# Cross-attention with a feed-forward block on one core: identity built by VectorE, output blocks in place, spread weight differences, and another order for x's loads and transposes

## Chip, cores and metric

The kernel runs on one core of one Trainium2 chip. The metric is the device time of one execution in microseconds (us), as a median of several executions. Beside it stands the span of the profiled execution, from its first to its last instruction; it is some 1.8 us shorter than the time of the same execution. PE is TensorE, PEld its weight load, DVE VectorE, ACT ScalarE, POOL GpSimd, SP SyncE. A run is called slow when its time is over 1.5% above the fastest of the same kernel; comparisons use the others. "Median" is that of all runs, slow ones too, unless it says otherwise.

## The reference, cut

```python
B, H, S, Ns, D = 8, 8, 512, 32, 64        # x: (B,H,S,D), state: (B,H,Ns,D)

def _attn_ref(x, state):
    scale = 1.0 / np.sqrt(D)
    a = softmax(scale * x @ state^T)       # S x Ns
    xread = a @ state
    a2 = softmax(scale * state @ x^T)      # Ns x S
    sread = a2 @ x
    return concatenate([xread, sread], axis=2)

def _moe_ref(x, w_in, w_out, s, b):        # 4352 tokens x 512, d_ff = 2048
    r = np.maximum(x @ w_in, 0.0)
    return (s * (r * r) + b) @ w_out
```

(The two softmaxes are abridged here. The output has (512 + 32) x 8 rows of 512 values.)

## The kernel before

The kernel goes through the batches in stages. In the stage of batch s, PE computes `h` of batch s in 16 blocks (f = 0 to 15), and between them the output products of batch s-1 and the scores `T` of batch s+1. The output product of a batch is a 2 x 2 block scheme with seven products instead of eight (`p` in the code), with sums and differences of weights (`wd`) and tokens (`s`) made by VectorE. Half of batch 0 (called `0b`) goes this way too. The transposes of x SP issues as DMAs, and the loads of x and stores of the output share POOL's queue.

```python
    upool = ctx.enter_context(tc.tile_pool(name="upool", bufs=1))   # qa, u2, u3, qb: one buffer each
    opool = ctx.enter_context(tc.tile_pool(name="opool", bufs=3))   # output blocks: three buffers
    ...
    def load_x(b):                      # on POOL's queue, f32 -> f16
        new_xn(b)
        nc.gpsimd.dma_start(out=xn[b]..., in_=x[b]...)

    def att_xT_dma(b):                  # on SP's queue; T of batch b reads xT
        xT = new_xT(b)
        nc.sync.dma_start_transpose(out=xT..., in_=xn[b]...)
    ...
        def put(bank, add, j, n0):
            ...
            else:
                osb = opool.tile([P, ni, NH], FP32, name=f"osb_{b}_{j}_{n0}", tag="osb")
            ...
                nc.vector.scalar_tensor_tensor(osb, acc[bank], s_bc, add, ALU.mult, ALU.add)
            ...
            nc.gpsimd.dma_start(dst[j][:, :, n0 : n0 + NH], osb)

        def done(p):
            ...
            elif p == 6:
                u = keep("u2")
                nc.vector.scalar_tensor_tensor(u, acc["B"], s_bc, kept["qa"], ALU.mult, ALU.add)
            ...
            elif p == 5:
                put("C", kept["u3"], 1, NH)
            elif p == 4:
                put("B", kept["qb"], 1, 0)
            else:
                put("C", kept["u2"], 0, NH)
    ...
        def pieces(s):                  # what goes behind block f of stage s
            nb = s + 1
            if s == 1:
                ...
                at(8, lambda: att_xT_dma(3))
                at(12, lambda: load_x(4))
                ...
            if s == 2:
                at(1, lambda: load_x(5))
            elif s in (3, 4):
                at(1, lambda: load_x(s + 3))
            if nb < B:
                ...
                ahead(4, lambda: att_T(nb, [0, 1]))
                ...
                if s in (2, 3):
                    at(6, lambda: att_xT_dma(nb + 1))
                at(9, lambda: att_a4_dma(nb))
                if s == 2:
                    at(9, stT_dma)
                elif s in (3, 4):
                    at(9, lambda: att_xT_dma(s + 3))
```

The softmax here doesn't subtract the row's maximum and nothing guards it: scores larger than these inputs give would overflow.

Of the kernel before, what the change touches and what calls it, by code (L numbers as in the profile page):

```python
# [10 lines left out]
FP16 = mybir.dt.float16  # L11
# [3 lines left out]
def kernel(  # L15
# [10 lines left out]
    nc = tc.nc  # L26
# [61 lines left out]

    warm = konst.tile([P, 512], FP16, name="warm")
    ident16 = konst.tile([P, P], FP16, name="ident16")  # L90
    ident_dr = nc.inline_tensor(np.eye(P, dtype=np.float16), name="ident_const")
    bones16 = konst.tile([P, P], FP16, name="bones16")
    ones16 = konst.tile([P, Ns], FP16, name="ones16")
    mean16 = konst.tile([P, P], FP16, name="mean16")
# [30 lines left out]
    def load_wi(c):  # L125
        nc.gpsimd.dma_start(
            out=wi[c],
            in_=moe_w_in.rearrange("(k p) f -> p k f", p=P)[:, :, c * FC : (c + 1) * FC],
        )
# [258 lines left out]
    def mm1_close(key, hps, ntok, f):  # L388
        if f % 2 == 0:
            R2[key] = rpool.tile([P, 2, ntok], FP16, name=f"r_{key}_{f}", tag="r")  # L390
        r16 = R2[key]
        if key == 0 and f in (1, 5):
            nc.vector.tensor_scalar(r16[:, f % 2], hps, 0.0, None, ALU.max)
        else:
            nc.scalar.activation(r16[:, f % 2], hps, AF.Relu)  # L395
            G["relu"] = nc.cur_bb.bb.instructions[-1]
        if f % 4 == 0:
            G4[key, f // 4] = gpool.tile([P, 4, ntok], FP16, name=f"g_{key}_{f}", tag="g")
        gt = G4[key, f // 4]
        G[key, f] = gt[:, f % 4]  # L400
        if key == 1 and f in (5, 9):
            with tc.issue_after(nc.cur_bb.bb.instructions[-1]):
                nc.scalar.square(gt[:, f % 4 - 1 : f % 4 + 1], r16)
        elif f % 2 == 1:
            nc.vector.tensor_mul(gt[:, f % 4 - 1 : f % 4 + 1], r16, r16)  # L405
            G["last"] = nc.cur_bb.bb.instructions[-1]
# [111 lines left out]
    def fast_items(b):  # L518
# [41 lines left out]
        def put(bank, add, j, n0):  # L560
            if b == "sr":
                ends.append(own[1][:, len(ends) : len(ends) + 1])
                osb = ends[-1]
            else:
                osb = opool.tile([P, ni, NH], FP32, name=f"osb_{b}_{j}_{n0}", tag="osb")
            if bank == "C" and b == last_b:
                for i in range(ni):
                    nc.vector.scalar_tensor_tensor(
                        osb[:, i], acc["C", i], s_bc, add[:, i], ALU.mult, ALU.add
                    )  # L570
            else:
                nc.vector.scalar_tensor_tensor(osb, acc[bank], s_bc, add, ALU.mult, ALU.add)  # L572
            if b == "sr":
                for i in range(4):
                    dst = out_BSn[4 * j + i, S:ST, n0 : n0 + NH]
                    eng = nc.sync if i % 2 else nc.scalar
                    eng.dma_start(dst, osb[Ns * i : Ns * i + Ns, 0])
                return
            if b == "0b":
                nc.gpsimd.dma_start(x_dst(0, 2 + j)[:, n0 : n0 + NH], osb[:, 0])  # L580
                return
            dst = out_BSn[b, 0:S].rearrange("(q ci cj) n -> cj q ci n", ci=2, cj=2)
            nc.gpsimd.dma_start(dst[j][:, :, n0 : n0 + NH], osb)  # L583
# [18 lines left out]
        def done(p):  # L602
            if p == 1:
                q = keep("qa")
                nc.vector.scalar_tensor_tensor(q, acc["A"], s_bc, blk(NH), ALU.mult, ALU.add)
            elif p == 6:
                u = keep("u2")
                nc.vector.scalar_tensor_tensor(u, acc["B"], s_bc, kept["qa"], ALU.mult, ALU.add)  # L608
            elif p == 2:
                put("A", blk(0), 0, 0)  # L610
            elif p == 7:
                u = keep("u3")
                nc.vector.scalar_tensor_tensor(u, acc["B"], s_bc, kept["qa"], ALU.mult, ALU.add)
                d = bias_d.unsqueeze(1).broadcast_to([P, ni, NH])
                with tc.issue_after(nc.cur_bb.bb.instructions[-1]):
                    nc.vector.tensor_add(keep("qb"), kept["qa"], d)
# [6 lines that stand above are left out]
# [35 lines left out]
    def bias_sum():  # L658
        ps = att_ps([P, DM], FP32, "wsum_ps")
        wsum = apool.tile([P, 2, DM], FP16, name="wsum", tag="W", bufs=1)  # L660
        for i in range(NKF // 4):
            for q in range(4):
                mm(
                    ps[32 * q : 32 * q + 32, :],
                    ones16,
                    wof(4 * i + q),
                    start=(i == 0),
                    stop=(i == NKF // 4 - 1),
                    tp=(0, 32 * q),
                )  # L670
        nc.vector.tensor_copy(wsum[:, 0], ps)
        nc.vector.tensor_sub(wsum[:, 1], ps, wsum[:, 0])
        A["wsum"] = wsum

    def bias_end():
# [34 lines left out]

    with tc.manual_schedule(engines={ET.PE, ET.SP, ET.Pool}):
        nc.vector.memset(warm, 0.0)
        nc.scalar.dma_start(ident16, ident_dr.ap())
        for g in range(NG):
            nc.sync.dma_start(
                xf[:, g],
                x[0, g :: NG].rearrange("h (q c) d -> q h (c d)", q=P),
            )
        nc.scalar.dma_start(stf[:, 0:2, :], st_v[:, 0:2, :])
        nc.scalar.preload_act_table_set("natural_log_exp_and_others")  # L720
        nc.sync.dma_start(stf[:, 2:4, :], st_v[:, 2:4, :])
        nc.sync.dma_start(sb_row[:, 0:1], moe_s.to_broadcast((1, 1)))
# [1 line left out]
        nc.gpsimd.memset(bones16, 0.0)  # L724
        for q in range(4):
            nc.gpsimd.memset(bones16[32 * q : 32 * q + 32, 32 * q : 32 * q + 32], 1.0)
        nc.gpsimd.memset(ones16, 1.0)
        nc.gpsimd.memset(mean16, 1.0 / Ns)
        nc.gpsimd.memset(one_row, 1.0)

        def cast_st(eng, b0, b1):
            n = 2 * (b1 - b0)
            src = stf[:, 2 * b0 : 2 * b1].unsqueeze(2).broadcast_to([P, n, 2, D])
            eng.tensor_copy(st16[:, 2 * b0 : 2 * b1], src)
# [9 lines left out]
        load_wi(0)  # L744
        load_wi(1)
        cast_st(nc.gpsimd, 0, 1)
        load_wi(2)
        cast_x0(1, 1, nc.gpsimd.tensor_copy)
        cast_st(nc.gpsimd, 1, 2)
# [4 lines left out]
        nc.gpsimd.dma_start(out=st16[:, 4:, 0, :], in_=st_v[:, 4:, :])  # L754
        load_x(2)

        warm_up(11)
        cast_x0(0, 0, nc.vector.tensor_copy)
        cast_x0(0, 1, nc.scalar.copy)
        att_xT_pe(0, 0)  # L760
        att_stT(0)
        cast_x0(1, 0, nc.vector.tensor_copy)
        warm_up(2)
        att_T(0, [0])
# [37 lines left out]
        def pieces(s):  # L802
# [30 lines left out]
                return out  # L833
            if s == 2:
                at(1, lambda: load_x(5))
            elif s in (3, 4):
                at(1, lambda: load_x(s + 3))
            if nb < B:
                if nb < NST:
                    at(0, lambda: att_stT(nb))  # L840
                ahead(4, lambda: att_M(nb, 0, "later"))
                ahead(4, lambda: att_T(nb, [0, 1]))
                ahead(4, lambda: att_M(nb, 1, "later"))
                at(4, lambda: att_ET(nb))
                at(4, lambda: A[nb]["M", 0]())
                at(6, lambda: A[nb]["M", 1]())
                at(8, lambda: att_shares(nb))
                if s in (2, 3):
                    at(6, lambda: att_xT_dma(nb + 1))
                at(9, lambda: att_a4_dma(nb))  # L850
                if s == 2:
                    at(9, stT_dma)
                elif s in (3, 4):
                    at(9, lambda: att_xT_dma(s + 3))
            if s == 2:
                at(1, lambda: att_srT_dma(0))
                at(8, lambda: att_V(1))
# [19 lines left out]
        for s in range(1, B):  # L877
# [16 lines left out]
            for f in range(NKF):  # L894
# [8 lines left out]
                    with tc.issue_after(G["last"]):  # L903
                        token_sum(s - 1, 4, f - 4)
                if s in fast:
                    if f in ((10, 12) if s == 1 else (7, 11)):
                        with tc.issue_after(G["last"]):
                            token_sum(s, 3, int(f > 10))
                    if s == 1 and f in (13, 14):
                        with tc.issue_after(G["last"]):  # L910
                            token_sum(s, f - 12, 0)
                    if s > 1 and f in (11, 12):
                        token_sum(s, f - 10, 0)
                    if f == 15:
                        token_sum(s, 1, 1)
                        token_sum(s, 2, 1)
                for fn in todo_s.get(f, []):
                    fn()
                if s == 1:
                    with tc.issue_after(G["last"]):  # L920
                        for _ in range({0: 2, 1: 1, 2: 1, 6: 1, 7: 1, 8: 1, 9: 1}.get(f, 0)):
                            sums.pop(0)()
                        for i, j in {0: [(1, 0), (2, 0)], 1: [(1, 1), (2, 1)], 7: [(3, 0)], 8: [(3, 1)],
                                     10: [(4, 0), (4, 1)]}.get(f, []):
                            token_sum("0b", i, j)
                for fn in items[f]:
                    fn()
        rest = coming[last_b][16:]
        rows = fast_items("sr")

# [53 lines left out]
```

## Time and profile before

| | before |
|---|---|
| time, median | 209.79 us (3 runs, 209.15 to 210.04) |
| span of the profiled run | 208.0 us |
| PE busy | 198.5 us, 95% |
| granted clock of TensorE | 1.0 but for the first stretch |
| losses of PE after the start, from start to start | 0.65 at 42.5, 0.70 at 48.1, 0.66 at 117.4 |

A loss "from start to start" is worked out here and below in one way: the time from the start of one matmul to the start of the next, less what such a pair takes when nothing waits. It comes out some 0.1 to 0.2 us above the wait that the profile prints, since that one counts from the modelled end of the matmul before. The prediction shows the lines.

### The profile page before, as it was taken

The numbers are of one execution on the slowest core, as the hardware profiler recorded it, in microseconds if no ns is written. First come the engines' busy times: TensorE is split into PE (matmuls) and PEld (weight loads), VectorE is DVE, ScalarE is ACT, GpSimd is POOL, SyncE is SP. The second block draws the span as 40 slices with busy tenths as digits, with TensorE's granted clock in tenths as the row PEclk, the third lists the DMA queues.
The fourth block names the chain that finished last, engine by engine and source line by source line (L and its number), as shares of the span: only waits on it lengthen the run. The fifth ranks groups of instructions, "written<-read, shape, count | busy, mean of one in ns | idle before, by whom it ended". The sixth has DMA issues, their size and how long they took to land.

```text
span 208.0 us, 4853 instructions
## 1 busy us (share of the span) xinstructions
PE 198.5 (95%) x1971; PEld 133.0 (64%) x1971; DVE 163.4 (79%) x286; ACT 128.5 (62%) x254; POOL 39.3 (19%) x66
## 2 busy tenths in 40 slices
PE   7988999998999999999999999999999999999991
PEld 2433333555766676667676667676767777788881
DVE  1479688987859996799779966997699786796861
ACT  2478966799577666767676658675957555543100
POOL 5690002413210230023002101120112012100210
PEclk9999999999999999999999999999999999999999
DMA  6999996997999397929961944160416011200243
GB/s 185 221 201 206 207 191 97 183 181 172 139 182 194 98 184 90 191 80 197 150 104 53 139 121 104 50 158 3 101 38 158 19 50 50 98 7 0 74 141 94
DMA packets 46795, 25.55 MB, mean 123 GB/s; under 512 B 31732, under 2 KB 44788, under 8 KB 46772
## 3 DMA queue, kind: packets, MB, share of 16 engines
q0 software_dynamic: 15568, 16.19, 39.8%
q1 hardware_dynamic: 30180, 8.49, 24.3%
q10 hardware_dynamic: 1024, 0.56, 1.0%
q8 instruction: 15, 0.25, 0.5%
q14 instruction: 8, 0.07, 0.2%
HBM read 17.33 MB, written 8.91 MB: 126 GB/s over the span
## 4 chain that ended last, share of the span: by engine, by line
PE 84%; DMA 5%; DVE 4%; ACT 3%; issue 1%; POOL 1%; ACTq 0%
PE h L70 24%; PE oB L70 18%; PE oC L70 11%; PE oA L70 11%; PE Mps L70 4%; PE o L70 3%; PE h_sr L70 3%; DMA stf<-in_state_dram 3%; DMA a<-aT 2%; ACT r L395 2%; PE V L70 1%; PE oB_sr L70 1%; PE T L70 1%; PE oB_0b L70 1%; PE oC_0b L70 1%
## 5 line engine op out<-in xcount | busy, mean ns | idle before, releaser
L395 ACT ACTIVATE r<-h 128x512 f16<-128x512 f32 x126 | 74.3, 602 | 45.0 <-PE h L70 45.0
L70 PE MATMUL h<-a,M 128*128 128x512 f16 x256 | 74.2, 379 | 1.4 <-DVE M L320 0.6
L70 PEld LDWEIGHTS <-s 128*128 128x128 f16 x448 | 43.7, 98 | 15.8
L405 DVE TENSOR_TENSOR g<-r 128x1024 f16<-128x1024 f16 x62 | 42.2, 683 | 12.8 <-ACT r L395 12.1
L70 PEld LDWEIGHTS <-g 128*128 128x128 f16 x392 | 37.2, 98 | 18.5 <-issue 4.4
L583 POOL DMA_DIRECT2D out_dram<-osb x27 | 18.3, 676 | 124.2 <-DVE osb L572 51.6
L70 PE MATMUL oB<-wd,s 128*128 128x256 f16 x224 | 32.8, 272 | 0.0
L70 PE MATMUL oA<-wo,g 128*128 128x256 f16 x224 | 32.5, 273 | 0.0
L70 PEld LDWEIGHTS <-M 128*128 128x128 f16 x256 | 24.3, 98 | 12.3 <-issue 2.1
L297 ACT CAST M<-Mps 128x1024 f16<-128x1024 f32 x20 | 20.1, 1007 | 0.0
L70 PE MATMUL oC<-wd,s 128*128 128x256 f16 x112 | 16.5, 273 | 0.0
L70 PE MATMUL oB<-wd,g 128*128 128x256 f16 x112 | 15.7, 273 | 0.0
L70 PE MATMUL oC<-wo,s 128*128 128x256 f16 x112 | 15.3, 273 | 0.0
L608 DVE SCALAR_TENSOR_TENSOR u<-oB,s_bc,qa 128x512 f32<-128x512 f32 x7 | 5.2, 749 | 7.6 <-PE oB L70 7.6
L395 ACT ACTIVATE r_sr<-h_sr 128x256 f16<-128x256 f32 x16 | 6.1, 383 | 7.9 <-PE h_sr L70 7.3
L234 ACT ACTIVATE E<-T 128x256 f16<-128x256 f32 x20 | 7.4, 385 | 4.0 <-PE T L70 4.0
L514 DVE TENSOR_TENSOR s<-s,g 128x1024 f16<-128x1024 f16 x14 | 9.6, 686 | 0.2
L70 PE MATMUL h_sr<-srdT,wi 128*128 128x256 f16 x64 | 9.6, 273 | 0.0
L516 DVE TENSOR_TENSOR s<-g,s 128x1024 f16<-128x1024 f16 x14 | 9.6, 685 | 0.0
L507 DVE TENSOR_TENSOR s<-g 128x1024 f16<-128x1024 f16 x14 | 9.6, 684 | 0.0
L512 DVE TENSOR_TENSOR s<-g,g 128x1024 f16<-128x1024 f16 x14 | 9.6, 683 | 0.0
L572 DVE SCALAR_TENSOR_TENSOR osb<-oC,s_bc,u 128x512 f32<-128x512 f32 x12 | 8.9, 745 | 0.4 <-PE oC L70 0.4
(126 smaller groups left out, 226.5 us busy)
## 6 DMA issues: line engine op xcount, KB each, us to landing
out_dram<-osb POOLq DMA_DIRECT2D x29, 256.0 KB, 2.8
xn<-in_x_dram POOLq DMA_DIRECT2D x7, 512.0 KB, 8.8
wi<-in_moe_w_in_dram POOLq DMA_DIRECT2D x4, 512.0 KB, 8.4
wo<-in_moe_w_out_dram POOLq DMA_DIRECT2D x4, 512.0 KB, 15.1
xf<-in_x_dram SPq DMA_DIRECT2D x2, 512.0 KB, 4.8
out_dram<-osb_0b POOLq DMA_DIRECT2D x4, 128.0 KB, 6.2
out_dram<-osb_sr SPq DMA_DIRECT2D x8, 32.0 KB, 1.6
out_dram<-osb_sr ACTq DMA_DIRECT2D x8, 32.0 KB, 1.7
```

The source lines that it names most:

```text
L70: return nc.tensor.matmul(out, lhsT, rhs, start=start, stop=stop, tile_position=tp, is_transpose=is_transpose, skip_group_check=True,)
L234: nc.scalar.activation(a["E"][:, g, 256 * m : 256 * m + 256], Ts[m][:, g, :], AF.Exp, scale=scale, accum_out=a["rs"][:, NG * m + g : NG * ...
L297: nc.scalar.copy(dst, ps)
L395: nc.scalar.activation(r16[:, f % 2], hps, AF.Relu)
L405: nc.vector.tensor_mul(gt[:, f % 4 - 1 : f % 4 + 1], r16, r16)
L507: nc.vector.tensor_sub(o, a11, a21)
L512: nc.vector.tensor_add(o, a21, a22)
L514: nc.vector.tensor_sub(o, SQ[b, 1, j], a11)
L516: nc.vector.tensor_sub(o, a12, SQ[b, 2, j])
L572: nc.vector.scalar_tensor_tensor(osb, acc[bank], s_bc, add, ALU.mult, ALU.add)
L583: nc.gpsimd.dma_start(dst[j][:, :, n0 : n0 + NH], osb)
L608: nc.vector.scalar_tensor_tensor(u, acc["B"], s_bc, kept["qa"], ALU.mult, ALU.add)
```

## The change

Its intent, as read from the diff: start sooner (no load of an identity matrix, state rows first on their queue); take the two early waits of PE away (batch 1's differences no longer stand in front of `u_0b`; an output block is written over its own addend instead of into one of three shared buffers); and move the transposes of x for batches 5 to 7 and the loads of x for batches 6 and 7 to other blocks.

```diff
-    ident_dr = nc.inline_tensor(np.eye(P, dtype=np.float16), name="ident_const")
+    lane_c, lane_r = ...                       # 0..31 down the lanes, and its transpose
...
-        if key == 1 and f in (5, 9):
+        if key == 1 and f in (3, 5):           # which square goes to ACT
...
                 osb = ends[-1]
+            elif bank != "A":
+                osb = add                      # in place, in u3, qb and u2
             else:
...
+                G["u2", b] = nc.cur_bb.bb.instructions[-1]
...
-        nc.scalar.dma_start(ident16, ident_dr.ap())
+        ... 12 VectorE instructions that build ident16 ...
+        nc.scalar.dma_start(stf[:, 0:2, :], st_v[:, 0:2, :])
...
-        warm_up(11)
+        warm_up(9)
+        att_stT(0)
+        warm_up(2)
...
-            elif s in (3, 4):
-                at(1, lambda: load_x(s + 3))
...
-                if s in (2, 3):
+                if s == 2:
                     at(6, lambda: att_xT_dma(nb + 1))
...
-                elif s in (3, 4):
-                    at(9, lambda: att_xT_dma(s + 3))
+                if s in (2, 3):
+                    at(15, lambda: load_x(s + 4))
+                if s in (3, 4, 5):
+                    at(9, lambda: att_xT_dma(s + 2))
...
-                        for _ in range({0: 2, 1: 1, 2: 1, 6: 1, 7: 1, 8: 1, 9: 1}.get(f, 0)):
+                        for _ in range({0: 2, 1: 1, 2: 1, 3: 1, 6: 1, 9: 1}.get(f, 0)):
...
+                if s == 1 and f == 8:
+                    with tc.issue_after(G["u2", "0b"]):
+                        sums.pop(0)()          # differences behind u2 and u3 of the half batch
...
```

(Cuts are marked by dots; the three constants that move behind the first cast of the state, and the rest of the new places of the differences, are left out.)

More of the change, by code (lines that the diff above doesn't have):

```diff
@@ L90 @@
     ident16 = konst.tile([P, P], FP16, name="ident16")
-    ident_dr = nc.inline_tensor(np.eye(P, dtype=np.float16), name="ident_const")
+    lane_c = konst.tile([P, 32], FP16, name="lane_c")
+    lane_r = konst.tile([P, 32], FP16, name="lane_r")
     bones16 = konst.tile([P, P], FP16, name="bones16")
@@ L613, in done @@
                 nc.vector.scalar_tensor_tensor(u, acc["B"], s_bc, kept["qa"], ALU.mult, ALU.add)
+                G["u3", b] = nc.cur_bb.bb.instructions[-1]
                 d = bias_d.unsqueeze(1).broadcast_to([P, ni, NH])
@@ L672, in bias_sum @@
         nc.vector.tensor_sub(wsum[:, 1], ps, wsum[:, 0])
+        G["last"] = nc.cur_bb.bb.instructions[-1]
         A["wsum"] = wsum
@@ L712 @@
         nc.vector.memset(warm, 0.0)
-        nc.scalar.dma_start(ident16, ident_dr.ap())
+        nc.vector.memset(lane_c[:, 0:1], 0.0)
+        for w in (1, 2, 4, 8, 16):
+            nc.vector.tensor_scalar_add(lane_c[:, w : 2 * w], lane_c[:, 0:w], float(w))
+        nc.vector.transpose(lane_r, lane_c)
+        nc.vector.memset(ident16, 0.0)
+        for q in range(4):
+            blk32 = slice(32 * q, 32 * q + 32)
+            nc.vector.tensor_tensor(
+                ident16[blk32, blk32], lane_c[blk32], lane_r[blk32], ALU.is_equal
+            )
+        nc.scalar.dma_start(stf[:, 0:2, :], st_v[:, 0:2, :])
         for g in range(NG):
@@ L718 @@
             )
-        nc.scalar.dma_start(stf[:, 0:2, :], st_v[:, 0:2, :])
         nc.scalar.preload_act_table_set("natural_log_exp_and_others")
@@ L726 @@
             nc.gpsimd.memset(bones16[32 * q : 32 * q + 32, 32 * q : 32 * q + 32], 1.0)
-        nc.gpsimd.memset(ones16, 1.0)
-        nc.gpsimd.memset(mean16, 1.0 / Ns)
-        nc.gpsimd.memset(one_row, 1.0)
         def cast_st(eng, b0, b1):
@@ L746 @@
         cast_st(nc.gpsimd, 0, 1)
+        nc.gpsimd.memset(one_row, 1.0)
+        nc.gpsimd.memset(mean16, 1.0 / Ns)
+        nc.gpsimd.memset(ones16, 1.0)
         load_wi(2)
@@ L760 @@
         att_xT_pe(0, 0)
-        att_stT(0)
         cast_x0(1, 0, nc.vector.tensor_copy)
@@ L905 @@
                 if s in fast:
-                    if f in ((10, 12) if s == 1 else (7, 11)):
+                    if f in ((12,) if s == 1 else (7, 11)):
                         with tc.issue_after(G["last"]):
@@ L920 @@
                     with tc.issue_after(G["last"]):
-                        for _ in range({0: 2, 1: 1, 2: 1, 6: 1, 7: 1, 8: 1, 9: 1}.get(f, 0)):
+                        for _ in range({0: 2, 1: 1, 2: 1, 3: 1, 6: 1, 9: 1}.get(f, 0)):
                             sums.pop(0)()
-                        for i, j in {0: [(1, 0), (2, 0)], 1: [(1, 1), (2, 1)], 7: [(3, 0)], 8: [(3, 1)],
-                                     10: [(4, 0), (4, 1)]}.get(f, []):
+                        for i, j in {0: [(1, 0), (2, 0)], 1: [(1, 1), (2, 1)], 3: [(3, 0)], 7: [(3, 1)]}.get(f, []):
                             token_sum("0b", i, j)
+                if s == 1 and f == 8:
+                    late_sum = sums.pop()
                 for fn in items[f]:
                     fn()
+                if s == 1 and f == 8:
+                    with tc.issue_after(G["u2", "0b"]):
+                        sums.pop(0)()
+                    sums.append(late_sum)
+                if s == 1 and f == 10:
+                    with tc.issue_after(G["u3", "0b"]):
+                        token_sum("0b", 4, 0)
+                        token_sum("0b", 4, 1)
+                        token_sum(1, 3, 0)
         rest = coming[last_b][16:]
```

## The prediction

> **What bounds the kernel now.** I read the page's table of engines, then busy time by window, then the waits of PE, and only then the timeline around each wait.
>
> ```profile
> PE 198.5 (95%) x1971; PEld 133.0 (64%) x1971; DVE 163.4 (79%) x286; ACT 128.5 (62%) x254; POOL 39.3 (19%) x66
> ...
> 62.00:83.00 21.00, 21.00 (x256) 14.65 (x254) 18.09 (x29) 14.47 (x33) 3.19 (x5) 1.00 0.82 142
> 125.00:146.00 21.00, 21.00 (x226) 14.66 (x224) 17.99 (x30) 14.51 (x31) 2.71 (x4) 1.00 0.30 78
> ```
>
> PE is busy all of 21 us in two windows (columns: length, then PE, PEld, DVE, ACT, POOL). One batch takes some 21.1 us, and the start-to-start times of its matmuls leave no room. So a gain can come only from PE's gaps. The waits of PE name three beyond the start:
>
> ```profile
> PE oC_0b L70 <- DVE osb_0b L572: 0.5, 1, 0.5
> PE h L70 <- DMA a<-aT: 0.5, 1, 0.5
> PE oB_0b L70 <- DVE u_0b L608: 0.5, 1, 0.5
> ```
>
> These are counted from the modelled end of the matmul before. From start to start I find 0.65, 0.70 and 0.66 us lost, at 42.5, 48.1 and 117.4 us: 2.0 us in all, 1.0% of the time. The rest of PE's idle time is the first 24 us and the tail after 204 us, and the tail is untouched. More than 2% (4.2 us) is out of reach.
>
> The timeline says what is behind the first two:
>
> ```profile
> 41.39 0.42 DVE L507 TENSOR_TENSOR s_0b<-g 128x512 f16<-128x512 f16 x1
> 41.73 0.68 DVE L490 TENSOR_TENSOR wd<-wo,wd 128x1024 f16<-128x1024 f16 x1
> ...
> 42.33 0.42 DVE L507 TENSOR_TENSOR s_0b<-g 128x512 f16<-128x512 f16 x1
> ...
> 42.67 0.48 DVE L608 SCALAR_TENSOR_TENSOR u_0b<-oB_0b,s_bc,qa_0b 128x256 f32<-128x256 f32 x1
> ...
> 43.20 0.60 PE L70 MATMUL oB_0b<-wd,s_0b 128*128 128x256 f16 x4 [0.48 <-DVE u_0b L608]
> ...
> 48.37 0.48 DVE L572 SCALAR_TENSOR_TENSOR osb_0b<-oC_0b,s_bc,u_0b 128x256 f32<-128x256 f32 x1 [1.04 <-PE oB_0b L70]
> ...
> 48.91 0.27 PE L70 MATMUL oC_0b<-wo,s_0b 128*128 128x256 f16 x1 [0.54 <-DVE osb_0b L572]
> ```
>
> The first: u_0b stands behind weight and token differences in VectorE's queue. The second: the matmul named as releaser is not the one osb_0b reads. That product ended at 46.6. In the compiled program this instruction waits for a POOL-queue DMA too, since it reuses an output buffer. The DMA view of the window around that issue gives it:
>
> ```profile
> out_dram<-osb POOLq DMA_DIRECT2D x2, 256.0 KB, 8.1
> ```
>
> Issued at 40.19, landed 8.1 us later, at 48.3: that is the wait.
>
> **What the Trainium skill says.** (1) "TensorE: Matmul & The Clock Gate", the section on 56 ns against 53.3 ns: start to start, a cold matmul of 512 columns takes 426.7 ns and a warm one 215.7. The trace agrees: the first warm-ups start 0.427 us apart, later ones 0.216. (2) "VectorE: DVE Perf Modes", the section on the TRN2 errata: a VectorE instruction has a fixed term of about 150 cycles, some 0.16 us. The trace agrees: the 128x1 copies took 0.16. (3) "DMA: Bandwidth & Descriptors", section "Queues, rings and completion order": each engine consumes a queue's descriptors in ring order. The trace agrees: outputs issued after the load of x at 49.68 landed after it, in order.
>
> **Part by part.**
>
> *Identity and state rows.* Added on VectorE: 12 small instructions, by 0.16 us some 1.9 us, between 1.1 and about 3.1; VectorE was idle until 4.93. This is free. A load of 32 KB goes. The state rows, first in ACT's queue, should land near 3.7 instead of 6.73.
>
> ```profile
> 5.86 1.06 PE L70 MATMUL xTps<-ident,xn 128*128 128x128 f16 x8
> 7.24 0.29 PE L70 MATMUL stTps<-ident,st 128*128 128x128 f16 x2 [0.32 <-POOL st L734]
> ...
> 7.91 0.30 PE L70 MATMUL T<-xT,stT 64*32 64x256 f16 x8
> ```
>
> T at 7.91 waited for stT (7.85). But two cold transposes now precede the eight of x: 2 x 0.107 = 0.21 us, so these end at 7.13 instead of 6.92. ACT's copy of 0.59 follows, to 7.75, and T starts near 7.80. Gain: 0.1 us, not the 3 us by which the rows arrive sooner. After it D, Ln, Exp and the casts of M hang on T one by one, so 0.1 is kept.
>
> *Differences spread.* In the compiled order u_0b (u2) now stands ahead of three of the instructions above. Its product ends at 41.4, so it runs from 41.4 to 41.9. PE reaches its next use at 42.56. The whole first gap goes: 0.6 us. In exchange ACT squares an earlier pair (1.06 us in a stretch where it had idled 1.13) and no longer the pair at 43.5, and VectorE takes that one back (0.6).
>
> *Output in place.* osb_0b no longer needs a buffer. It now stands behind a square that waits for ACT: E ends near 46.25, relu at 46.75, square to 47.4, reciprocal 0.15, then the output to about 48.0. PE is ready at 47.6 in the new time. So of 0.70 about 0.3 goes.
>
> *x loads.* The compiled order of POOL's queue is unchanged: the load of x for batch 6 stood directly behind an output already and ran at 74.95. Nothing gained. On SP the transposes of x for batches 5 to 7 each come a batch later, always directly behind that of a. The stage with the third gap keeps the same neighbours. I read the late transpose there as held up by an instruction fetch of 16 KB at 116.07 (0.93 us on one DMA engine), which comes at a fixed place of PE's program, so it may return. I count half: 0.3.
>
> Sum so far: 0.1 + 0.6 + 0.3 + 0.3 = 1.3 us, 208.5.
>
> **Rivals.** First, a wait that takes the place. The in-place outputs of the half batch lie in the buffers named u2, u3 and qb, of which there is one each. Batch 1 writes the same ones, and in the compiled program its u2 now waits for the DMA of the half batch's last output.
>
> ```profile
> out_dram<-osb_0b POOLq DMA_DIRECT2D x1, 128.0 KB, 7.1
> ...
> 58.27 0.75 DVE L608 SCALAR_TENSOR_TENSOR u<-oB,s_bc,qa 128x512 f32<-128x512 f32 x1 [1.35 <-PE oB L70]
> ...
> 59.83 0.49 PE L70 MATMUL oB<-wd,s 128*128 128x256 f16 x3
> ```
>
> Issued at 52.94, landed 7.1 later at 60.04; u2 ran at 58.27. If that landing stays, u2 ends at 60.8 and PE's oB starts at 60.85 instead of 59.83. This pins the time, whatever was gained before: 1.0 us later, less 0.3 for the third gap, gives 210.5. For it: the output queues behind a load of x, which started its packets only after the transpose of x had ended at 51.5, and that transpose waits for a load that landed at 47.65. None of this depends on PE. Against it: POOL gets to that load about 1 us sooner. If it slips ahead of the transpose, the output may land by 58 and nothing is lost. In later batches the output of u2 lands 2.6 us before its next use in batch 2, in batch 3 only 0.1; PE has about 0.8 us of slack there.
>
> Second, the start is hidden: if the state rows or x land later because both queue at once, PE's order (warm-up, state, x) makes x wait for state. Worth up to 0.3 us the wrong way.
>
> Third, everything lands well: both gaps go whole, the late a is gone, no new wait: 2.1 us, 207.7.
>
> **Range and chances.** I give the pinned case (210.5, in part 209.5) a little over half, and the free case (208.5, at best 207.7) the rest. The middle is 209.3. The runs of before spread from 209.15 to 210.04, so 0.4 us either way is noise. Range 207.9 to 210.8. Faster or slower by over 2% needs 4.2 us, more than all gaps together: 0.01 each, within 2%: 0.98.
>
> **What would show it.** Right: the waits of PE no longer list u_0b at 42 us; T starts at 7.8; osb_0b's successor runs before 48.1; VectorE idles before the u of batch 1 until a DMA lands near 60, and oB of batch 1 shows a gap of 1 to 2 us. Wrong: u runs at 57 with no wait (then the third rival), T stays at 7.9 or comes at 7.4, a new gap at 117 or none, or a gap in the stage of batch 5 where the transpose of x moved. A time under 207.7 would mean that the first 24 us hold a gain that I did not see.

## The result, and the profile after

The changed kernel took **211.94 us** (median of 6 runs, 211.02 to 212.29); the kernel before, beside it, 209.91 us (6 runs, 209.15 to 210.31). The ratio is 1.0094, with a 95% interval of 1.0066 to 1.0122: within 2%, and slower. A ratio is the mean time of one kernel's fast runs over that of the other's of the same rounds, so it is not quite the ratio of the medians quoted here. The profiled run has a span of 210.2 us against 208.0, at a granted clock of 1.0. PE is busy for 198.3 us, where it was 198.5. All of the 2.2 us is waiting.

The waits of PE in the changed kernel (columns: us in total, times, longest), beside those of before in the prediction:

```profile
PE T L70 <- DMA xT<-xn: 1.5, 2, 0.8
...
PE oB L70 <- DVE u L611: 0.6, 1, 0.6
...
PE h L70 <- DMA a<-aT: 0.5, 1, 0.5
...
PE oC_0b L70 <- DVE u_0b L575: 0.3, 1, 0.3
```

`u_0b` of line 608 is gone, and the wait at 48 us is smaller. The late `a` is where it was. Two lines are new, T for xT and oB for `u`, 2.1 us together.

From start to start:

| where in the changed kernel | waits for | loss, us | before |
|---|---|---|---|
| 42 | `u_0b` | none | 0.65 |
| 47.2 | `osb_0b`, now in place in `u_0b` | 0.51 | 0.70 |
| 57.6 | T of batch 3, for its xT | 0.95 | none |
| 59.7 | oB of batch 1, for `u` | 0.74 | none |
| 101.9 | T of batch 5, for its xT | 0.88 | none |
| 113.2 | oC, for `u` | 0.29 | none |
| 119.2 | h, for `a` | 0.66 | 0.66 |
| 145.9 | T of batch 7, for its xT | 0.29 | none |

The sum is 4.31 against 2.00. Less the 0.2 us gained at the start, that is 2.1 us of the 2.2 us between the spans. Of these, 0.67 us are there when PE's oB of batch 1 starts (60.50 us instead of 59.83); the rest comes after it.

**The parts that did what was wanted.** The start, in the timeline of the changed kernel:

```profile
5.57 0.29 PE L70 MATMUL stTps<-ident,st 128*128 128x128 f16 x2 [0.35 <-POOL st L746]
...
7.69 0.30 PE L70 MATMUL T<-xT,stT 64*32 64x256 f16 x8 [0.53 <-DVE xT L198]
```

T starts 0.22 us sooner (it was 7.91). That is one pair of profiles: over all the kept ones T starts at 7.52 to 8.07 us in the six with the old start and at 7.48 to 7.75 in the ten with the new one, so a gain of 0.2 is no larger than the spread. VectorE in the stage of batch 1:

```profile
41.23 0.48 DVE L611 SCALAR_TENSOR_TENSOR u_0b<-oB_0b,s_bc,qa_0b 128x256 f32<-128x256 f32 x1 [0.24 <-PE oB_0b L70]
...
46.65 0.69 DVE L406 TENSOR_TENSOR g<-r 128x1024 f16<-128x1024 f16 x1
47.26 0.15 DVE L337 RECIPROCAL rq<-rs 128x2 f32<-128x2 f32 x1
47.33 0.46 DVE L575 SCALAR_TENSOR_TENSOR u_0b<-oC_0b,s_bc,u_0b 128x256 f32<-128x256 f32 x1
```

`u_0b` runs as soon as its product is there, and the output in place waits for no DMA any more; it runs behind a square and a reciprocal, 1.0 us sooner than `osb_0b` did.

**The stage of batch 2, which holds batch 1's output products and the scores of batch 3.** The timeline around 58 us, three lines out of many:

```profile
58.73 0.44 PE L70 MATMUL T<-xT,stT 64*32 64x256 f16 x16 [0.78 <-DMA xT<-xn]
...
59.70 0.75 DVE L611 SCALAR_TENSOR_TENSOR u<-oB,s_bc,qa 128x512 f32<-128x512 f32 x1 [3.83 <-DMA out_dram<-u_0b]
...
60.50 0.49 PE L70 MATMUL oB<-wd,s 128*128 128x256 f16 x3 [0.57 <-DVE u L611]
```

VectorE stands still for 3.83 us. `u` of batch 1 wants the buffer from which the half batch's last output is still being stored; that store landed at 59.60. PE's oB comes at 60.50 instead of 59.83. In the kernel before, this output landed no sooner, at 60.09; but there it lay in a buffer of its own, and no `u` waited for it. T of batch 3 had waited just before. Both waits hang on the load of x on POOL's queue. Before, and after:

```profile
49.68 0.91 POOL L120 DMA_DIRECT2D xn<-in_x_dram  x1
```

```profile
48.62 0.92 POOL L121 DMA_DIRECT2D xn<-in_x_dram  x1
...
51.73 0.55 POOL L583 DMA_DIRECT2D out_dram<-u_0b  x1 [1.64 <-DVE u_0b L575]
```

This is the load of x for batch 4. SP's transpose for batch 3 starts within 0.2 us of the same time in both (47.78 and 47.65). In the changed kernel the load follows it 1.0 us after, where it had been 1.9 us. The transpose landed at 58.69 instead of 54.10. Its 256-byte packets had gone by 52; its last ones, 32 packets of 4 bytes, came only from 55 on, among the 512-byte packets of the load (before: from 51.7 to 52.4, with the load's first at 52.1). The output behind the load landed at 59.60.

**The stage of batch 4.** SP's transposes of x for batch 5, before and after:

```profile
83.84 3.69 SPq L204 DMA_TRANSPOSE xT<-xn  x1
```

```profile
93.92 4.11 SPq L205 DMA_TRANSPOSE xT<-xn  x1
```

T of batch 5 needs it at about 102. The slack was 18 us; now it is 8. Before, this transpose landed 5.4 us after its issue. The transpose for batch 6 stood at 93.33 then, beside the same load of x, and T of batch 6 read it only at 123. Now the load of x for batch 7 (issued at 96.95) is under way with it. The DMA view of the changed kernel from 99.5 to 102 us, by queue (packets, MB, time of the packets as a share of 16 engines):

```profile
q0 software_dynamic: 691, 0.47, 121.2%
q1 hardware_dynamic: 28, 0.00, 1.5%
```

q1, the transposes' queue, has 28 packets of almost no bytes left to send, and q0 is full with the load. T started at 102.97.

So the theory, called A in the expectations: the change removes waits of PE, but makes transposes of x wait for loads of x on the other queue, and `u` of batch 1 for an output that stands behind such a load. Rivals: one part of the change is a loss by itself (in place, or the loads of x late), or the losses are where they were only by chance.

### The profile page after: what moved, and what is told of

Its sections match the earlier page's. It is cut to its first block, busy times and chain, and to the rows that moved or that the text cites. A ratio compares the mean times of both kernels' runs of the same rounds, so it can differ in the third digit from the quotient of the medians.

```text
span 210.2 us, 4863 instructions
## 1 busy us (share of the span) xinstructions
PE 198.3 (94%) x1971; PEld 132.5 (63%) x1971; DVE 165.4 (79%) x298; ACT 128.5 (61%) x254; POOL 39.0 (19%) x66
## 4 chain that ended last, share of the span: by engine, by line
PE 49%; issue 19%; DMA 16%; ACT 5%; DVE 4%; POOL 4%; SPq 0%; POOLq 0%; DVEq 0%
PE h L70 13%; PE oB L70 9%; DMA xT<-xn 8%; PE oC L70 7%; PE oA L70 4%; PE o L70 3%; PE h_sr L70 3%; DMA ET<-E 3%; DMA xf<-in_x_dram 3%; DMA a<-aT 2%; ACT r L396 2%; PE Mps L70 2%; POOL out_dram L586 2%; PE oB_sr L70 1%; POOL xn L121 1%
## 5 line engine op out<-in xcount | busy, mean ns | idle before, releaser
L586 POOL DMA_DIRECT2D out_dram<-u x13 | 8.8, 677 | 54.3 <-DVE inv L281 26.1
L586 POOL DMA_DIRECT2D out_dram<-osb x7 | 4.7, 671 | 60.7 <-DVE rt L336 22.0
```

## The experiments

All were correct and ran in four groups, each on one chip beside the kernel before (medians of before: 209.44, 209.94, 209.43, 210.01). Names that start with a are the changed kernel with something undone or moved; names that start with b are the kernel before with something added. The chips differ, so runs of different groups are compared by their ratios.

| run | median, us | lowest to highest (runs) | median of the fast runs (their number) | ratio of fast runs to before, 95% |
|---|---|---|---|---|
| a_oldx | 209.82 | 208.83 to 215.05 (6) | 209.58 (5) | 1.003, 0.9997 to 1.0063 |
| a_ownout | 211.69 | 210.21 to 214.25 (6) | 210.49 (4) | 1.0093, 1.0044 to 1.0142 |
| b_xlate | 213.30 | 211.58 to 213.46 (6) | 213.30 (6) | 1.0185, 1.0152 to 1.0218 |
| b_inplace | 212.13 | 209.39 to 215.43 (6) | 211.12 (3) | 1.0073, 1.0028 to 1.0119 |
| a_xt6 | 212.16 | 209.22 to 215.00 (8) | 210.02 (4) | 0.9982, 0.9916 to 1.0049 |
| a_x4 | 211.40 | 210.74 to 213.60 (6) | 211.40 (6) | 1.0099, 1.0046 to 1.0152 |
| a_oldx_x4 | 208.60 | 208.19 to 209.23 (6) | 208.60 (6) | 0.9946, 0.9908 to 0.9984 |
| b_spread | 210.84 | 209.67 to 213.54 (6) | 209.84 (4) | 1.0024, 0.9969 to 1.0079 |
| b_x4 | 209.28 | 208.77 to 210.02 (6) | 209.28 (6) | 0.9985, 0.9950 to 1.0020 |
| a_xt6_x4 | 208.65 | 208.47 to 209.32 (6) | 208.65 (6) | 0.9951, 0.9916 to 0.9985 |
| a_own0b | 212.48 | 211.17 to 214.86 (6) | 212.38 (5) | 1.0126, 1.0081 to 1.0171 |
| b_ident | 209.27 | 209.03 to 209.95 (6) | 209.27 (6) | 0.9988, 0.9954 to 1.0022 |
| a_x4_x7 | 209.95 | 209.06 to 211.18 (6) | 209.95 (6) | 1.0001, 0.9960 to 1.0041 |
| b_inplace_x4 | 209.19 | 208.67 to 209.91 (6) | 209.19 (6) | 0.9962, 0.9925 to 0.9998 |

### a_oldx: the changed kernel with the old places of x's loads and transposes

```diff
-                if s in (2, 3):
-                    at(15, lambda: load_x(s + 4))
-                if s in (3, 4, 5):
-                    at(9, lambda: att_xT_dma(s + 2))
+                elif s in (3, 4):
+                    at(9, lambda: att_xT_dma(s + 3))     # and the other lines as before
```

> The changed kernel with the old order of x loads and x transposes; all else stays. Theory A (the loss is a sum of new DMA waits, of which the transposes of x moved to just before their use make the waits of T at 101.9 and 145.9 us): these two waits go (0.80 + 0.20 us beyond the usual 0.09), the 0.29 us at 113.2 with them, the wait of T at 57.6 and of oB at 59.7 stay: some 210.7 us. Rival B (what I predicted: the order of the x transposes does nothing, and all of the loss is the pinned u2): unchanged, 211.9 us.

The ratio is 1.003, against 1.0094: the new places cost some 1.3 us by these ratios, and the other three parts together still gain nothing. The profile fell in a slow run of 215.05 us and can't be set against fast ones. It shows something else. Timeline, then windows (length, busy time of PE, PEld, DVE, ACT, POOL with counts, granted clock, DMA share, GB/s):

```profile
61.81 0.80 PE L70 MATMUL oB<-wd,s 128*128 128x256 f16 x3 [3.05 <-DVE u L611]
```

```profile
61.60:68.00 6.40, 6.19 (x26) 3.53 (x26) 3.78 (x9) 2.15 (x4) 0.67 (x1) 0.54 1.13 202
```

Here the output landed later still, at 60.91, PE stood for 3 us, and then the granted clock was 0.54 for 6 us. The page "TensorE: Matmul & The Clock Gate" of the Trainium skill, section "What's actually happening", says that TensorE falls to half its clock after an idle window of about 3.4 us. The trace agrees in kind, though this pause was 3.05 us. T of batch 3 did not wait here, against what was expected: its transpose landed at 57.51, just in time. The program of this kernel and that of the changed one are the same up to about 80 us, so how late that output lands differs from run to run. From start to start the wait of oB is 0.74 us in one profile and 3.22 in the other, and the half clock comes on top.

### a_ownout: the changed kernel with output buffers of its own

```diff
-            elif bank != "A":
-                osb = add
```

> The changed kernel with the half batch's and later outputs in buffers of their own again; all else stays. Theory A: the waits of T (0.85) and oB (0.74) at 57.6 and 59.7 us both go, as the load of x for batch 4 is issued a microsecond later again, behind a later output; but oC_0b waits until near 48.9 us for the landing of the first outputs again, so that what was gained before that point is lost: oB of batch 1 starts near 59.9 as in the kernel before, 211.2 us in all. Rival B (only the buffer of u2 counts, the wait of T comes from the order of the DMAs as such): oB's wait goes, T's wait stays at 0.85 us.

The ratio, 1.0093, is that of the changed kernel. In the profile both waits near 58 and 60 are gone, and the wait at 47 for an output buffer is back (0.71 from start to start). T of batch 5 still waits:

```profile
PE T L70 <- DMA xT<-xn: 0.9, 1, 0.9
```

From start to start T of batch 5 lost 1.12 us and the late `a` 0.90, more than in the changed kernel, so the time gained before went into these waits. The pair at 58 to 60 us comes with in place output, and the wait at 102 comes from elsewhere.

### b_xlate: the kernel before with the new places of x's loads and transposes alone

The edit is that of a_oldx the other way round, on the kernel before.

> The kernel before with the new order of x loads and x transposes alone. Theory A: T of batch 5 and of batch 7 wait for their x: 0.8 to 1.3 us more, 210.9 us, with nothing different before 80 us. Rival B: 209.9, unchanged.

213.30 us, the slowest of all. This part alone is a loss of 1.85%, with an interval that ends just above 2%. The timeline:

```profile
103.95 0.44 PE L70 MATMUL T<-xT,stT_all 64*32 64x256 f16 x16 [1.51 <-DMA xT<-xn]
```

1.68 us from start to start, against 0.88 in the changed kernel. Four of the six runs (213.2 to 213.5 us) had a granted clock of 0.988 or 0.989; the two with 0.995 and 1.0 took 211.58 and 212.53. The direction is as theory A has it; the size is larger than the wait alone. In the profiled run part of it lies at 48 us, where nothing was changed: oC_0b waited 1.33 us from start to start, against 0.70 before, since the earlier output landed at 49.03 and not at 48.25. A lowered clock would add to it, but where those four runs lost their clock no profile shows.

### b_inplace: the kernel before with in place output alone

```diff
+            elif bank != "A":
+                osb = add
```

> The kernel before with the outputs in place alone. Theory A: the gap at 48.1 us goes (some 0.6 us) and the load of x for batch 4 is issued that much sooner, so the transpose of x for batch 3 lands later and u2 of batch 1 waits for an output to land near 59.6 to 60.1; oB of batch 1 starts near 60.5 to 60.9 instead of 59.83: 0.7 to 1.0 us slower, 210.7. Rival C (the new waits come only because the spread differences and the start run ahead of the DMAs): 209.3, faster by the gap.

212.13 us, from 209.39 to 215.43, three of six runs slow; the three fast ones have a ratio of 1.0073. The profile is of a slow run; its waits of PE begin with

```profile
PE oB L70 <- DVE u L610: 2.5, 1, 2.5
```

In this run the output landed at 60.87, and the clock was 0.60 from 61.7 to 66. In place alone takes the gap at 48 away and puts the wait at 59 in its place, with a size that differs from run to run.

### a_xt6: the changed kernel with the transposes for batches 5 to 7 issued after block 6 instead of block 9

```diff
                 if s in (3, 4, 5):
-                    at(9, lambda: att_xT_dma(s + 2))
+                    at(6, lambda: att_xT_dma(s + 2))
```

> The changed kernel with one difference: the transposes of x for batches 5 to 7 are issued a third of a batch earlier (after block 6 instead of after block 9); the loads of x stay where the change put them. Theory A (the transposes of x now end just as T needs them): the waits of T for xT of batches 5 and 7 go, 0.8 + 0.2 us, and the time is about 210.9 against 211.9 for the changed kernel, its span about 209.2 against 210.2. T of batch 3 still waits about 0.8 and oB of batch 1 about 0.7. Rival B (the place on the queue of transposes decides little; the load of x for batch 7, issued at the end of a stage, is what holds up the transposes): T of batch 5 still waits 0.5 to 1 us and the time stays at 211.9. Rival C (the loss is only in batch 1's stage): no change in time.

Four of eight runs were slow, and the profile is of one (a wait of 3.4 us of oB for `u`, then 7.5 us at a clock of 0.63). No T waits for xT in it, that of batch 3 neither, which was expected to. The transpose for batch 5 is issued 4.8 us before that in the changed kernel although PE runs some 5 us later, so the move is worth about half a batch. The fast runs, 209.22 to 211.44, have a ratio of 0.9982, against 1.0094 for the changed kernel. Theory A holds for batches 5 and 7; the wait near 60 us is unmended, and it is what the profiled slow run shows.

### a_x4: the changed kernel with the load of x for batch 4 behind the half batch's outputs

```diff
-                at(12, lambda: load_x(4))        # in stage 1
...
             if s == 2:
+                at(0, lambda: load_x(4))
                 at(1, lambda: load_x(5))
```

> The changed kernel with the load of x for batch 4 moved on the POOL queue from between the half batch's outputs to behind them. Theory A (in place output frees that queue 1 us sooner, so the load of x for batch 4 collides with the transpose for batch 3, and with the half batch's last output, which u2 of batch 1 waits for): the output of u_0b lands by 56, T of batch 3 and oB of batch 1 don't wait, 0.86 + 0.65 = 1.5 us off: about 210.4; the waits of T for xT of batches 5 and 7 stay. Rival B (the output lands late because of its own writes, or of the load of x for batch 5): u2 still waits for a landing near 59 and the time stays near 211.9. Rival C (the transpose itself takes 11 us whatever runs beside it): T of batch 3 still waits 0.8.

The last output of the half batch now landed at 57.1 and the transpose for batch 3 at 54.4, and both waits near 58 and 60 are gone, as theory A has it. All the kept profiles agree. Where the load follows the transpose for batch 3 by 1.9 us or more (eleven of them), that transpose lands 5.6 to 6.9 us after its issue; where by 0.7 to 1.6 us (five), 8.8 to 11.0 us. The half batch's last output lands at 59.0 to 61.6 us in the ten profiles in which the load stands before it on POOL's queue, the kernel before among them, and at 54.3 to 57.2 in the six in which it stands behind.

The time is 211.40, 1.0 above what theory A expected. The gain was given back in the stage of batch 4:

```profile
102.56 0.44 PE L70 MATMUL T<-xT,stT_all 64*32 64x256 f16 x16 [1.88 <-DMA xT<-xn]
```

In the changed kernel T had started at 102.97. PE came 1.6 us sooner to the place and waited for nearly the same landing: 2.06 us from start to start. The wait is pinned to a DMA, so what is gained upstream turns into waiting.

### a_oldx_x4: both repairs

The edits of a_oldx and a_x4 together; spread differences, in place output and the new start stay.

> The changed kernel with the old order of the transposes and loads of x, and the load of x for batch 4 behind the half batch's outputs: both repairs at once, in place and spread differences kept. Theory A: what is left is the 0.5 at 47 us and the late a at 117 to 119 (0.65); start 0.22 and the first gap 0.65 and 0.2 at the second gained: about 208.6 to 208.9 against 209.5 before, ratio 0.995 to 0.998, no pause near 58 us and so no run at a lowered clock. Rival B (PE pauses near 58 whatever is moved): 209.8 or over, with single runs of 213 to 215.

**208.60 us**, ratio 0.9946, as expected, and it is faster than both kernels. No run was slow: 208.19 to 209.23. Windows from 57 to 62 us, the changed kernel and this one:

```profile
57.00:62.00 5.00, 3.65 (x54) 2.24 (x53) 2.30 (x4) 2.60 (x11) 0.00 (x0) 1.00 1.44 160
```

```profile
57.00:62.00 5.00, 5.00 (x66) 3.38 (x64) 3.06 (x7) 4.05 (x12) 0.69 (x1) 1.00 1.53 177
```

PE is busy all of the 5 us again, at a full clock, with a DMA share that is no smaller. What is left is 0.51 at 47.3 and 0.45 at 116.4 from start to start.

### b_spread: the kernel before with the differences spread, nothing else

> The kernel before with batch 1's weight and token differences spread, nothing else. Theory A: the gap of 0.65 us at 42.5 goes, but the next wait at 48 us is for an output buffer whose DMA lands at 48.2 whatever PE did before, so that wait grows by as much: time unchanged, 209.3 to 209.6, and the wait of oC_0b for osb_0b 1.0 to 1.3 us from start to start. Rival B (the gains add): 208.8, ratio 0.997, with the gap at 48 us still 0.7.

210.84 us (209.84 without the slow runs), ratio 1.0024 with an interval that holds 1. The gap at 42.5 is gone, and this line is what became of it:

```profile
48.56 0.27 PE L70 MATMUL oC_0b<-wo,s_0b 128*128 128x256 f16 x1 [1.22 <-DVE osb_0b L572]
```

1.39 us from start to start, against 0.70: the two gaps of before in one, a little over the 1.0 to 1.3 that theory A expected. The buffer that `osb_0b` waits for came free at 47.9, when its DMA landed (48.25 before). The gains do not add: alone, spreading gains nothing here.

### b_x4: the control, the kernel before with only the load for batch 4 moved

> The kernel before with the load of x for batch 4 behind the half batch's outputs on the POOL queue, nothing else: the control of the fastest version so far (208.6). Theory A: before, no wait of PE hangs on that load (the outputs have buffers of their own, T of batch 3 doesn't wait), so nothing changes: ratio 0.998 to 1.002, gaps of 0.65, 0.7 and about 0.65 to 1.0 us as before. Rival B (the moved load is a gain by itself, and the change's four parts give nothing): about 208.8, ratio 0.996.

Ratio 0.9985, interval 0.995 to 1.002, and three gaps of 2.08 us together, where before has 2.00. No gain of the moved load by itself is shown, so the gain of a_oldx_x4 should come from the parts of the change that it lets through. The two intervals overlap; the ledger of gaps says it more clearly: 0.96 us are left in a_oldx_x4, 2.08 here.

### a_xt6_x4: both repairs, with the late loads kept

The edits of a_xt6 and a_x4 together.

> The changed kernel with the transposes of x for batches 5 to 7 after block 6 and the load of x for batch 4 behind the half batch's outputs; the late loads of x stay. Theory A: both repairs suffice, no T waits for xT, u2 doesn't wait: as with the old x order, 208.4 to 209.0, ratio 0.993 to 0.998. Rival B (the late loads themselves cost): 209.5 to 210.5, with T of batch 5 or 7 still waiting for xT.

208.65 us, ratio 0.9951, as good as a_oldx_x4. No T waits for xT. With the transpose for batch 5 issued at 83.04 us, the new places of the loads cost nothing that shows. Rival B falls.

### a_own0b: the changed kernel, one output of the half batch in a buffer of its own

```diff
-            elif bank != "A":
+            elif bank != "A" and (b, bank, j) != ("0b", "C", 0):
                 osb = add
```

> The changed kernel with one difference: the last output of the half batch (the one that lies in u2) gets a buffer of its own again; everything else in place. Theory A (u2 of batch 1 waits for that output's DMA because of the shared buffer): u2 runs at once, oB of batch 1 doesn't wait (0.65 us off), T of batch 3 still waits for xT if the load of x for batch 4 still collides (about 0.8), T of batch 5 still waits (0.8 to 2). Time 210.8 to 211.4, ratio about 1.006 to 1.008. Rival B (something else holds oB at 59 to 60): the wait stays and the time too.

The wait of oB for `u` is gone, from one buffer, though the output landed at 60.05: `u` ran at 57.05 all the same. This is the direct proof that the shared `u2` caused it. T of batch 3 waits on (0.64 from start to start), and T of batch 5 for 1.52. Both are in one line of PE's waits:

```profile
PE T L70 <- DMA xT<-xn: 1.8, 2, 1.4
```

The time, 212.48 us, misses the expected 210.8 to 211.4. The profiled run, at 211.17, was the lowest. T's waits lie within what was expected or just below it; why the other fast runs took up to 213.56, two of them at granted clocks of 0.988 and 0.992, is not explained.

### b_ident: the kernel before with the new start alone

> The kernel before with the identity built by VectorE and the state rows first, nothing else. Theory A: T starts 0.2 us sooner, the gap at 42.5 stays 0.65, and osb_0b still waits for its buffer, whose DMA lands at about 48.2: the gap at 48 grows from 0.7 to 0.9 and nothing is gained: ratio 0.999 to 1.001. Rival B: 0.2 us is kept, ratio 0.999, gap at 48 still 0.7 (times alone can't tell it; the gap can). Rival C (the start costs because x lands later): T later than 7.9.

Ratio 0.9988, interval 0.9954 to 1.0022: nothing that these times can tell. T started at 7.50. The profiled run had a stretch at half clock from 11.7 to 15.1 us, so PE came about 1 us late to the gap at 48, where the buffer was already free. What that gap would have been otherwise can't be read here. Inconclusive on the pin, clear on the time.

### a_x4_x7: as a_x4, and the load of x for batch 7 moved away from the transpose for batch 5

```diff
-                if s in (2, 3):
-                    at(15, lambda: load_x(s + 4))
+                if s == 2:
+                    at(15, lambda: load_x(6))
+                elif s == 4:
+                    at(8, lambda: load_x(7))
```

> The changed kernel with the load of x for batch 4 behind the half batch's outputs and the load of x for batch 7 moved from the end of a stage (issued at 95 to 97) to behind the first output of the next one (about 104). The transposes of x for batches 5 to 7 stay where the change put them. Theory A1 (the transpose for batch 5 is late only because its last packets, the 4-byte ones that report it done, queue behind the load for batch 7; alone such a transpose landed 5.4 us after its issue): it lands by 99.5, T of batch 5 doesn't wait, the span is about 207.3 and the time 208.8 to 209.1 (ratio 0.996 to 0.998). Theory A2 (the transpose is simply issued too late, 8 us before use, whatever runs beside it): T of batch 5 still waits 0.9 to 2 us, time 210.5 to 211.4.

T of batch 5 doesn't wait, though its transpose is issued at 92.29, as late as in a_x4 (92.33). So the late issue alone does no harm; with the load of x beside it, it does (A1). But the time is 209.95, not 208.8 to 209.1, since the load, now issued at 103.36, met another transpose. VectorE's timeline:

```profile
109.56 1.22 DVE L279 TENSOR_REDUCE den<-ET 128x32 f32<-128x1024 f16 x1 [1.29 <-DMA ET<-E]
```

ET's transpose took 7.0 us to land, `u` stood behind `den`, and PE lost 0.70 us at 110.7. The cost went from one transpose to the next.

### b_inplace_x4: in place alone, without the load in between

The edits of b_inplace and a_x4 on the kernel before.

> The kernel before with output in place and the load of x for batch 4 behind the half batch's outputs, nothing else: in place without the collision. Theory A (in place is a gain, and the collision is what made it a loss): the gap at 48 us falls from 0.7 to 0.1 to 0.3 (the spread differences are not there, so PE comes 0.6 later), no wait at 58 to 62 us, no run at a lowered clock: 208.8 to 209.2, ratio 0.995 to 0.999. Rival B (in place costs something else as well): 210 or over, or a pause of PE near 59 us.

209.19 us, ratio 0.9962, where b_inplace had 212.13 and 1.0073. No run was slow, the gap at 48 us is under 0.2 from start to start, and PE has no pause near 59. In place is then a small gain (the interval ends just under 1). What made it a loss is the load of x ahead of the half batch's last output, for which `u` of batch 1 now waits.

## Why the prediction was wrong

- **Start**: 0.22 us instead of 0.1 in this pair, within the spread of T's start. The sum behind the 0.1 was off in its parts: the state rows landed at 4.98 us and not near 3.7, and PE's eight transposes of x took 0.61 us and not the 1.06 of a cold start. The second rival was right that x would be later (it landed at 5.25 instead of 4.91), wrong that T would be. No gain by itself shows in the times (b_ident).
- **Differences spread**: the first gap went whole, as said. b_spread shows that without in place output it comes back some 5 us later in the kernel.
- **In place**: 0.2 us of the 0.70 went, where 0.3 was said; the square and reciprocal ahead of it were named rightly.
- **First rival**: right in mechanism and nearly in size. The landing was predicted at 60.04 and was 59.60; oB was predicted at 60.85 and was 60.50. It had been given only a little over half. It missed a second wait from the same collision, T of batch 3, which, however, falls in the time before that same oB and adds little to it. The argument against it, that POOL reaches the load sooner and the output might land by 58, failed: the load ran sooner, but behind the transpose's data, so it held up that transpose's last packets (11.0 us to landing instead of 6.3) and the output hardly gained.
- **The step that failed** is "*x loads.*": "Nothing gained. On SP the transposes of x for batches 5 to 7 each come a batch later, always directly behind that of a. The stage with the third gap keeps the same neighbours." I looked only at what the move does to its neighbours on the queue, not at who reads the result and when. ("A batch later" is so for batches 6 and 7; for batch 5 it was 10 us, half a batch.) The transpose for batch 5 went from 83.84 to 93.92, with T due at 102, beside a load of x. T of batch 5 lost 0.88, T of batch 7 0.29, and the 0.29 at 113 came behind it: 1.5 us that no case of the prediction held, though its list of signs named a gap where the transpose of x moved. b_xlate (ratio 1.0185), a_xt6_x4 and a_x4_x7 show it from three sides.
- **Third gap**: 0.66 at 119.2, whole, where half was counted. It stayed in every fast profile, from 0.30 to 1.02, and its cause was not tested.

Put together: the rival's 210.5, with the pin 0.35 sooner, the third gap whole (0.3 more) and the missed 1.5 us, makes 211.9; measured was 211.94. That it fits so closely is luck, with runs 1.3 us apart. The top of the range, 210.8, was the first rival with nothing missed.

What stays open: why the half batch's output lands at 59.6 in one run and 61.6 in another (a_xt6) of the same program up to there, and where the runs of b_xlate and a_own0b with a lowered clock lost it. The late `a` near 117 was not tried.

## What to carry to other kernels

When a DMA is moved, ask two questions: when its reader needs it, and what runs on the other queues while it runs. A queue that comes free sooner may let a large load start beside a transfer that something waits for; here that transfer's last packets then came 3 us later. Writing in place spares a buffer, but ties the next writer of that buffer to the store's landing, so put the store ahead of loads on its queue. A gain ahead of a wait that a DMA ends is only worth something if that DMA moves too.

## What the Trainium skill lacked or had wrong

- "DMA: Bandwidth & Descriptors", section "Queues, rings and completion order", says that each engine takes turns between queues, packet by packet, and also that the write which raises a DMA's semaphore lands only after every earlier write of that engine, whichever queue it came from. So the direction of what was seen here is in the page; what it lacks is the size. In the changed kernel the transpose for batch 3 landed 11.0 us after its issue beside a load of 512 KB, its 256-byte packets gone by 52 us and its 4-byte packets sent from 55 on; in the kernel before, 6.3 us. The move of that load alone (a_x4) brought it to 6.7.
- The same page, in "Latency and other measured facts", gives 261 GB/s for a DMA transpose with a non-contiguous middle dimension, from one kernel, and more for the contiguous case. Here the transpose of x, from SBUF to SBUF in 256-byte packets, moved 209 GB/s from 49 to 49.9 us in the kernel before, when no other queue moved anything. Which of the page's two cases this is was not settled.
- "TensorE: Matmul & The Clock Gate", section "What's actually happening", gives an idle window of about 3.4 us for the fall of the clock. Here less was enough. Pauses of PE of 3.05 us (a_oldx) and 3.4 us (a_xt6) came with 6.8 us at half clock, one of 2.5 us (b_inplace) with 3.4 us; one of 1.9 us (a_x4) with none. In b_ident the clock was halved from 11.7 to 15.1 us with no pause of PE over 0.5 us since its first matmul. In a_oldx the 6.8 us at half clock are, as an estimate from that length alone, 3.4 us of work lost, about as much again as the pause.
